# A six-layer cross network: the first layer's second half fed by a DMA transpose and multiplied in column tiles

## The chip, the cores and the metric

The kernel runs on one core of a Trainium2 chip. Five engines work side by side, each with its own queue: TensorE (PE in the profile, with PEld for its weight loads), VectorE (DVE), ScalarE (ACT), GpSimd (POOL) and SyncE (SP), which here only issues transfers. The metric is the time of one execution in microseconds of the device; the time before is a median of 130.95 us over 3 runs (130.82 to 131.1).

## The reference, cut to what matters

There are B = 4096 rows of D = 416 features (bf16), and L = 6 layers, each with a 416 x 416 matrix and a bias:

```
x = x0
for l in range(6):
    x = x0 * (x @ ws[l] + bs[l]) + x
return x
```

Each layer needs all of the layer before, so the layers come one after another, but the 4096 rows are independent of each other.

## The kernel before, in words

**Layout.** 416 features are 3 blocks of 128 and a remainder of 32. The kernel holds x transposed: in `XM`, the partitions are the features of one block and the free dimension is the 4096 rows. `XM[0]` is x0 and stays; `XM[1]` and `XM[2]` take turns. The remainder's 32 features of 4 groups of 512 rows are stacked on the 128 partitions of `XR`; `XRd` is a copy of it with the two halves of the partitions swapped, for products that would otherwise meet on the same rows of TensorE's array. The 4096 rows are two halves (`s` = 0 and 1), each of four groups (`g`) of 512 columns. The main weights are in `WM`, the remainder's rows of them in `WR` (four copies, one in each 32 partitions), and their 32 x 32 corners on a diagonal in `WD`.

**A product.** For layers 1 to 4, `mm_full` (L177) makes one 128 x 512 block of the result from three 128-feature blocks; it splits the 128 output features into four column tiles of 32 (`tile_position=(0, 32*q)`), so a group of four matmuls (L181) fills the array. `mm_row` (L185) adds the remainder's 32 input features with row tiles (L187), and `mm_rem` (L191) makes the remainder's 32 output features with column tiles (L193 for the diagonal corner, L198 for the main blocks). The first layer uses a `full` of its own (L211) that does the same as `mm_full` with single 128 x 128 matmuls (L214), and a `row` (L217, its matmul at L221) that reads `XRd` for the second block (m = 1).

**After a product.** `ew_main` (L162) adds the bias on ScalarE (L165) from PSUM to a scratch tile `t`, multiplies by x0 (L166) and adds x (L169) on VectorE. `ew_rem` (L171) does the same for the remainder (L173 to L175). PSUM is one pool of four buffers, each of two banks: a new product can start only when ScalarE has emptied one. The framework orders each engine's work mostly as the program text has it; `pin` and `keep_in_program_order` hold an operation at its place in the text.

**The first layer, `first_layer(s)` (L208), run for s = 0 and then s = 1.** First the products of groups 0 and 1 for the three feature blocks (`pa`), then their row products and the one that opens the next tile (eight matmuls, which need `XR` and, for m = 1, `XRd`), then groups 2 and 3 (`pb`) and the last four row products, then the remainder product `pr`. Between the two halves, `x0_rem(1, ...)` (L155) transposes the second half's remainder on TensorE (four matmuls against the identity, L157) into the free bank of `pr`, and VectorE copies it to `XR` and, swapped, to `XRd` (three copies, L160).

**How the inputs come.** SP's queue issues, in this order: the transposed loads of x0's first two groups (L76, a DMA transpose of 512 rows x 384 features each), the remainder's weights for layer 0 (L88), groups 2 and 3, group 0 of the second half, the second half's remainder `xrem` (L85, rows of 64 bytes), groups 1, 2 and 3 of the second half, and then the weights of the other layers (L72, L91) and x0 by rows (L125). ScalarE's queue issues layer 0's weights, the biases and the first half's remainder (`xrig`, L81). ScalarE copies `WR` twice (L110) and GpSimd once (L112); GpSimd fills `WD` (L131) and regroups `xrem` into `xrig` (L134), so that a transpose of 128 x 128 blocks brings the four groups where `XR` has them.

**Layers 1 to 4** run over six tiles (half, feature block) in pairs, with the remainder pair for both halves (`rem_pair`, L267) after the first pair. **The last layer** turns the product round: the 128 rows of a block are the stationary operand and the 416 features the moving one (`mm_q_full`, L325, its matmul at L327), so that the result comes out by rows; `mm_q_rem` (L330) adds the remainder (L333) and the bias (L336). Two blocks of 128 rows are opened ahead of the first bias product, then the rest follows in four rounds. ScalarE takes the result from PSUM (L354), VectorE multiplies by x0 (L355) and adds x (L344), and SP writes it out.

Of the kernel before, what the change touches and what calls it, by code (L numbers as in the profile page):

```python
# [11 lines left out]
BF16 = mybir.dt.bfloat16  # L12
# [4 lines left out]
def kernel(  # L17
# [65 lines left out]
    def load_xrem1():  # L83
        with nc.allow_non_contiguous_dma(reason="64B row segments"):
            nc.sync.dma_start(xrem[:], x0_v[:, 16:32, NK * P:D])  # L85
# [29 lines left out]
    load_x0t(1, 0)  # L115
    load_xrem1()
    for g in range(1, NG):
        load_x0t(1, g)
    load_wm(nc.sync, 1)
# [13 lines left out]
    fill_wd(0, 1)  # L133
    nc.gpsimd.tensor_copy(xrig[:, 1].rearrange("p i (g r) -> p i g r", g=NG), xrem[:].rearrange("p (g i) r -> p i g r", g=NG))  # L134
    fill_wd(1, L)
# [19 lines left out]
    def x0_rem(s, tpr):  # L155
        for i in range(4):
            nc.tensor.transpose(tpr[:, 128 * i:128 * i + 128], xrig[:, s, i, :], ident[:])  # L157
        for dst, src in ((slice(0, P), slice(0, P)), (slice(64, P), slice(0, 64)), (slice(0, 64), slice(64, P))):
            to = XR[0] if dst == src else XRd
            nc.vector.tensor_copy(to[dst, CW * s:CW * s + CW], tpr[src])  # L160
# [46 lines left out]

    def first_layer(s):  # L208
        cur, curR, nxt, nxtR = XM[0], XR[0], XM[1], XR[1]

        def full(pt, m, h, gl, after_row):  # L211
            c0 = col0(s, 2 * h + gl)
            for k in range(NK):
                nc.tensor.matmul(pt[:, gl, :], lhsT=WM[:, 0, k, 128 * m:128 * m + 128], rhs=cur[:, k, c0:c0 + CW],  # L214
                                 start=(k == 0 and not after_row), stop=(k == NK - 1 and after_row))
# [13 lines left out]
        if s == 0:  # L229
            for m in range(NK):  # L230
                full(pa[m], m, 0, 0, False)
            tp0 = psum.tile([P, CW], BF16, tag="ps", name="tpr")
            x0_rem(0, tp0[:])
            for m in range(NK):
                full(pa[m], m, 0, 1, False)
        else:
            for m in range(NK):
                for gl in range(2):
                    full(pa[m], m, 0, gl, False)
        pb = [ph(0)]  # L240
# [6 lines left out]
        for m in range(NK):  # L247
            if m:
                pb.append(ph(m))
            for gl in range(2):  # L250
                full(pb[m], m, 1, gl, m == 0)
        row(pb[1], 1, 1, False)
        row(pb[2], 2, 1, False)
        pr = psum.tile([P, 2, CW], FP32, tag="ps", name="pr")
        mm_rem(0, s, pr[:, 0, :], cur, curR)
        if s == 0:
            x0_rem(1, pr[:, 1, :].bitcast(BF16)[:, 0:CW])
        for m in range(NK):
            ew_main(0, s, m, 1, pb[m], cur, nxt, pin=(s == 0))
        ew_rem(0, s, pr[:, 0, :], curR, nxtR)  # L260

    bias_setup()
# [3 lines left out]

    def rem_pair(l, cur, curR, nxtR, feeds_last):  # L267
        pr2 = psum.tile([P, 2, CW], FP32, tag="ps", name="pr2")
        for s in range(NS):
            mm_rem(l, s, pr2[:, s, :], cur, curR)  # L270
        for s in range(NS):
            ew_rem(l, s, pr2[:, s, :], curR, nxtR)
            if feeds_last:
                nc.sync.dma_start_transpose(out=scrR[s][:], in_=nxtR[:, CW * s:CW * s + CW])
# [50 lines left out]
    def mm_q_full(q, g, py, closes):  # L325
        for k in range(NK):
            nc.tensor.matmul(py[:, 0:D], lhsT=cur[:, k, q_cols(q, g)], rhs=WM[:, l, k, :],  # L327
                             start=((not closes) and k == 0), stop=(closes and k == NK - 1))
# [34 lines left out]
    for q, at, done in rounds:  # L363
# [7 lines left out]
        for u in range(done):  # L371
            mm_q_full(q, u, bank[u], False)
# [40 lines left out]
```

## Time and profile before

| | |
|---|---|
| runs | 130.95 us median (130.82 to 131.1, 3 runs) |
| the profiled execution | 130.71 us, span 128.9 us, granted clock 0.998 |
| TensorE | 123.1 us busy (96% of the span), 1690 matmuls |
| VectorE | 107.1 us busy (83%) |
| ScalarE | 86.9 us busy (67%) |
| GpSimd | 5.9 us busy (5%) |
| transfers | 16.37 MB in 42102 packets, over 90% busy from about 3 to 38 us |

The span is the time from the first to the last instruction that the profiler saw; the execution's own time is 1.8 us longer. All times in the text are microseconds from the start of the span. The busy share of TensorE counts pipelined matmuls and is no measure of the array at its peak. The chain that ended last follows the execution back from its last instruction, at each step to what released it; it is the view to read for what a change is worth, since an engine's work beside the chain costs nothing.

### The profile page before, as it was taken

Reading aid. Unit: us, or ns where it says so; the run is one execution under the profiler, and the core shown is the slowest. Engines: PE = TensorE matmul, PEld = TensorE weight load, DVE = VectorE, ACT = ScalarE, POOL = GpSimd, SP = SyncE. Lnnn points to the kernel's source line nnn. Section 1 sums busy time; section 2 is a strip of 40 time slices with the busy share of each in tenths; the row PEclk is TensorE's granted clock in tenths of the full one; section 3 lists DMA queues with packets and bytes.
Section 4 is the critical chain, followed back from the end, with each engine's and each line's share of the span. In section 5 each row is a group of like instructions: output and inputs, shape, how many; then the busy total and the mean of one; then the engine's idle time right before and its main releaser. Section 6 shows DMA issues by size and latency. Waiting matters only on the chain.

```text
span 128.9 us, 3973 instructions
## 1 busy us (share of the span) xinstructions
PE 123.1 (96%) x1690; PEld 54.9 (43%) x1690; DVE 107.1 (83%) x197; ACT 86.9 (67%) x99; POOL 5.9 (5%) x18
## 2 busy tenths in 40 slices
PE   6999999999999999999999999999999999999960
PEld 2343443354444444444444444444444445445420
DVE  1032979999999898989898989898989899898991
ACT  0426783987848577848668848668847896569670
POOL 4022200600000000000000000000000000000000
PEclk9999999999999999999999999999999999999999
DMA  3999999999990000000000000000297999995754
GB/s 106 237 203 217 170 158 260 247 328 333 336 299 11 5 0 8 0 0 5 0 5 0 5 0 5 0 5 0 42 166 164 123 219 178 187 323 188 231 179 139
DMA packets 42102, 16.37 MB, mean 127 GB/s; under 512 B 30906, under 2 KB 42084, under 8 KB 42084
## 3 DMA queue, kind: packets, MB, share of 16 engines
q1 hardware_dynamic: 39416, 15.56, 54.6%
q10 hardware_dynamic: 2668, 0.56, 2.3%
q8 instruction: 13, 0.21, 0.7%
q14 instruction: 5, 0.04, 0.1%
HBM read 6.15 MB, written 3.41 MB: 74 GB/s over the span
## 4 chain that ended last, share of the span: by engine, by line
PE 80%; DMA 8%; DVE 5%; issue 2%; SPq 1%; ACT 1%; DVEq 0%
PE pt L181 49%; PE ph L214 9%; DMA XM<-in_x_dram 8%; PE py L327 8%; PE pt L187 5%; PE pr L198 5%; DVE t L355 3%; DVE o L344 2%; PE pr L193 2%; SPq L76 1%; PE py L333 1%; PE ph L221 1%; PE py L336 1%; ACT t L354 1%; PE pr L157 0%
## 5 line engine op out<-in xcount | busy, mean ns | idle before, releaser
L181 PE MATMUL pt<-XM,WM 128*32 128x512 bf16 x1152 | 65.2, 379 | 0.0
L165 ACT ACTIVATE t<-pt,bM 128x1024 bf16<-128x1024 f32 x48 | 49.6, 1115 | 18.3 <-PE pt L187 18.3
L166 DVE TENSOR_TENSOR t<-t,XM 128x1024 bf16<-128x1024 bf16 x60 | 41.4, 690 | 5.3 <-ACT t L165 5.3
L169 DVE TENSOR_TENSOR XM<-t,XM 128x1024 bf16<-128x1024 bf16 x60 | 41.8, 696 | 3.4
L181 PEld LDWEIGHTS <-WM 128*32 128x32 bf16 x1152 | 29.7, 97 | 33.8 <-issue 5.1
L354 ACT CAST t<-py 128x416 bf16<-128x416 f32 (+1 forms) x23 | 14.8, 642 | 4.8 <-PE py L327 2.1
L327 PE MATMUL py<-WM,XM 128*128 128x416 bf16 x96 | 17.7, 340 | 0.0
L214 PE MATMUL ph<-XM,WM 128*128 128x512 bf16 x72 | 16.5, 379 | 0.1
L165 ACT ACTIVATE t<-ph,bM 128x1024 bf16<-128x1024 f32 x12 | 12.5, 1114 | 4.4 <-PE ph L221 4.4
L327 PEld LDWEIGHTS <-XM 128*128 128x128 bf16 x96 | 9.0, 98 | 8.5 <-issue 1.4
L355 DVE TENSOR_TENSOR t<-t,X0rows 128x416 bf16<-128x416 bf16 (+1 forms) x23 | 10.4, 454 | 1.2 <-ACT t L354 1.2
L214 PEld LDWEIGHTS <-WM 128*128 128x128 bf16 x72 | 6.8, 98 | 8.6 <-issue 1.3
L344 DVE TENSOR_TENSOR o<-t,XLrows 128x416 bf16<-128x416 bf16 (+1 forms) x23 | 10.3, 451 | 0.0
L173 ACT ACTIVATE t<-pr,bR 128x512 bf16<-128x512 f32 x10 | 6.4, 684 | 2.7 <-PE pr L198 2.1
L198 PE MATMUL pr<-XM,WM 128*32 128x512 bf16 x120 | 8.2, 379 | 0.0
L187 PE MATMUL pt<-XR,WR 32*128 32x512 bf16 x96 | 7.3, 379 | 0.0
L141 PE MATMUL wps<-warm 128*128 128x512 bf16 (+1 forms) x11 | 4.4, 593 | 1.2 <-DVE warm L94 1.2
L175 DVE TENSOR_TENSOR XR<-t,XR 128x512 bf16<-128x512 bf16 x10 | 4.2, 423 | 0.7
L198 PEld LDWEIGHTS <-WM 128*32 128x32 bf16 x120 | 3.2, 97 | 3.1
L106 ACT ACT_TABLE_LOAD x1 | 1.3, 1283 | 4.3 <-DMA WM<-in_ws_dram 4.3
L174 DVE TENSOR_TENSOR t<-t,XR 128x512 bf16<-128x512 bf16 x10 | 4.2, 418 | 0.0
L152 DVE CAST bM<-pb 128x18 f32<-128x18 bf16 x1 | 0.2, 177 | 4.6 <-PE pb L151 4.6
(39 smaller groups left out, 33.6 us busy)
## 6 DMA issues: line engine op xcount, KB each, us to landing
X0rows<-in_x_dram SPq DMA_DIRECT2D x4, 832.0 KB, 11.6
out_dram<-o SPq DMA_DIRECT2D x9, 208.0 KB, 2.4
WM<-in_ws_dram SPq DMA_DIRECT2D x5, 312.0 KB
out_dram<-o SPq DMA_DIRECT2D x13, 104.0 KB, 1.7
WR<-in_ws_dram SPq DMA_DIRECT2D x4, 130.0 KB, 4.1
WM<-in_ws_dram ACTq DMA_DIRECT2D x1, 312.0 KB
XM<-in_x_dram SPq DMA_TRANSPOSE x8, 4.9
xrig<-in_x_dram ACTq DMA_DIRECT2D x4, 32.0 KB, 4.1
```

Of the source, the lines that this page charges most:

```text
L165: nc.scalar.activation(t[:], pt[:].rearrange("p a b -> p (a b)"), ACT.Identity, bias=bM[:, m, l:l + 1], scale=1.0)
L166: prod = nc.vector.tensor_tensor(out=t[:], in0=t[:], in1=XM[0][:, m, c0:c0 + 2 * CW], op=ALU.mult)
L169: nc.vector.tensor_tensor(out=nxt[:, m, c0:c0 + 2 * CW], in0=t[:], in1=cur[:, m, c0:c0 + 2 * CW], op=ALU.add)
L173: nc.scalar.activation(tr[:, 0:CW], pr, ACT.Identity, bias=bR[:, l:l + 1], scale=1.0)
L181: nc.tensor.matmul(pts[g // 2][32 * q:32 * q + 32, g % 2, :], lhsT=WM[:, l, k, 128 * m + 32 * q:128 * m + 32 * q + 32], rhs=cur[:, k, c0:c ...
L187: nc.tensor.matmul(pts[g // 2][:, g % 2, :], lhsT=WR[32 * g:32 * g + 32, l, 128 * m:128 * m + 128], rhs=curR[32 * g:32 * g + 32, CW * s:CW ...
L198: nc.tensor.matmul(pr[32 * g:32 * g + 32, :], lhsT=WM[:, l, k, NK * P:D], rhs=cur[:, k, c0:c0 + CW], start=False, stop=(k == NK - 1), tile ...
L214: nc.tensor.matmul(pt[:, gl, :], lhsT=WM[:, 0, k, 128 * m:128 * m + 128], rhs=cur[:, k, c0:c0 + CW], start=(k == 0 and not after_row), sto ...
L327: nc.tensor.matmul(py[:, 0:D], lhsT=cur[:, k, q_cols(q, g)], rhs=WM[:, l, k, :], start=((not closes) and k == 0), stop=(closes and k == NK ...
L344: tc.keep_in_program_order(nc.vector.tensor_tensor(out=o, in0=t, in1=xl, op=ALU.add))
L354: nc.scalar.copy(tv, src)
L355: tc.keep_in_program_order(nc.vector.tensor_tensor(out=tv, in0=tv, in1=X0rows[:, b, :], op=ALU.mult))
```

## The change

It touches only the first layer, the order of some transfers and the last layer's first products:

- `xrem` is issued on ScalarE's queue instead of SP's.
- The second half's remainder is transposed by a DMA from SBUF to SBUF, issued on SP after group 2 of the second half and ahead of group 3, straight into `XR[0]`; TensorE's four transposes and VectorE's copy to `XR` go. GpSimd's regrouping copy moves ahead of its fills of `WD`. The two copies into `XRd` stay on VectorE, pinned ahead of the product of the first half's third tile (`x0_rem1`).
- The second half's products (s = 1) use `mm_full`, that is, four column tiles for each single matmul.
- The two remainder products of the first layer are made together, by `rem_pair`, in the second half after the first tile of groups 2 and 3; `rem_pair` itself is the same and only stands earlier in the text.
- The elementwise work on the first half's groups 2 and 3 is emitted in the second half, after the first tile's products.
- In the last layer, the first two blocks of the first round are multiplied with the stationary 128 columns split into four column tiles of 32.

```diff
@@ -82,7 +82,7 @@
 
     def load_xrem1():
         with nc.allow_non_contiguous_dma(reason="64B row segments"):
-            nc.sync.dma_start(xrem[:], x0_v[:, 16:32, NK * P:D])
+            tc.keep_in_program_order(nc.scalar.dma_start(xrem[:], x0_v[:, 16:32, NK * P:D]))
 
     def load_wr0():
         nc.sync.dma_start(WR[0:R, 0, :], ws[0, NK * P:D, :])
@@ -112,10 +112,13 @@
             nc.gpsimd.tensor_copy(dst, src)
     for g in range(2, NG):
         load_x0t(0, g)
-    load_x0t(1, 0)
     load_xrem1()
-    for g in range(1, NG):
+    for g in range(NG - 1):
         load_x0t(1, g)
+    nc.gpsimd.tensor_copy(xrig[:, 1].rearrange("p i (g r) -> p i g r", g=NG), xrem[:].rearrange("p (g i) r -> p i g r", g=NG))
+    nc.sync.dma_start_transpose(out=XR[0][:, CW:2 * CW].rearrange("p (i c) -> p i c", i=4),
+                                in_=xrig[:, 1].rearrange("p i c -> p (i c)"))
+    load_x0t(1, NG - 1)
     load_wm(nc.sync, 1)
     for g in range(NG):
         load_wr(nc.sync, g, 1, L)
@@ -130,9 +133,8 @@
         for g in range(NG):
             nc.gpsimd.tensor_copy(WD[32 * g:32 * g + 32, l0:l1, g, :], WR[32 * g:32 * g + 32, l0:l1, NK * P:D])
 
-    fill_wd(0, 1)
-    nc.gpsimd.tensor_copy(xrig[:, 1].rearrange("p i (g r) -> p i g r", g=NG), xrem[:].rearrange("p (g i) r -> p i g r", g=NG))
-    fill_wd(1, L)
+    for l0, l1 in ((0, 1), (1, L)):
+        fill_wd(l0, l1)
 
     wps = psum.tile([P, CW], FP32, tag="ps", name="wps")
 
@@ -152,12 +154,18 @@
         nc.vector.tensor_copy(bM[:], pb[:, 0:NK, 0:L])
         nc.vector.tensor_copy(bR[:], pb[:, 3, 0:L])
 
-    def x0_rem(s, tpr):
+    HALVES = ((slice(64, P), slice(0, 64)), (slice(0, 64), slice(64, P)))
+
+    def x0_rem0(tpr):
         for i in range(4):
-            nc.tensor.transpose(tpr[:, 128 * i:128 * i + 128], xrig[:, s, i, :], ident[:])
-        for dst, src in ((slice(0, P), slice(0, P)), (slice(64, P), slice(0, 64)), (slice(0, 64), slice(64, P))):
-            to = XR[0] if dst == src else XRd
-            nc.vector.tensor_copy(to[dst, CW * s:CW * s + CW], tpr[src])
+            nc.tensor.transpose(tpr[:, 128 * i:128 * i + 128], xrig[:, 0, i, :], ident[:])
+        nc.vector.tensor_copy(XR[0][:, 0:CW], tpr)
+        for dst, src in HALVES:
+            nc.vector.tensor_copy(XRd[dst, 0:CW], tpr[src])
+
+    def x0_rem1():
+        for dst, src in HALVES:
+            tc.keep_in_program_order(nc.vector.tensor_copy(XRd[dst, CW:2 * CW], XR[0][src, CW:2 * CW]))
 
     def ew_main(l, s, m, h, pt, cur, nxt, pin=False):
         c0 = col0(s, 2 * h)
@@ -205,10 +213,22 @@
         nc.sync.dma_start_transpose(out=XLrows[:, 16 * s:16 * s + 16, 128 * k:128 * k + 128],
                                     in_=nxt[:, k, SW * s:SW * s + SW])
 
+    def rem_pair(l, cur, curR, nxtR, feeds_last):
+        pr2 = psum.tile([P, 2, CW], FP32, tag="ps", name="pr2")
+        for s in range(NS):
+            mm_rem(l, s, pr2[:, s, :], cur, curR)
+        for s in range(NS):
+            ew_rem(l, s, pr2[:, s, :], curR, nxtR)
+            if feeds_last:
+                nc.sync.dma_start_transpose(out=scrR[s][:], in_=nxtR[:, CW * s:CW * s + CW])
+
     def first_layer(s):
         cur, curR, nxt, nxtR = XM[0], XR[0], XM[1], XR[1]
 
         def full(pt, m, h, gl, after_row):
+            if s == 1:
+                mm_full(0, s, m, 2 * h + gl, {h: pt}, cur, not after_row, after_row)
+                return
             c0 = col0(s, 2 * h + gl)
             for k in range(NK):
                 nc.tensor.matmul(pt[:, gl, :], lhsT=WM[:, 0, k, 128 * m:128 * m + 128], rhs=cur[:, k, c0:c0 + CW],
@@ -230,13 +250,18 @@
             for m in range(NK):
                 full(pa[m], m, 0, 0, False)
             tp0 = psum.tile([P, CW], BF16, tag="ps", name="tpr")
-            x0_rem(0, tp0[:])
+            x0_rem0(tp0[:])
             for m in range(NK):
                 full(pa[m], m, 0, 1, False)
         else:
             for m in range(NK):
                 for gl in range(2):
                     full(pa[m], m, 0, gl, False)
+                if m == 0:
+                    for mm in range(NK):
+                        if mm == 2:
+                            x0_rem1()
+                        ew_main(0, 0, mm, 1, late[mm], cur, nxt, pin=True)
         pb = [ph(0)]
         row(pa[0], 0, 0, False)
         row(pb[0], 0, 1, True)
@@ -249,29 +274,21 @@
                 pb.append(ph(m))
             for gl in range(2):
                 full(pb[m], m, 1, gl, m == 0)
+            if s == 1 and m == 0:
+                rem_pair(0, cur, curR, nxtR, False)
         row(pb[1], 1, 1, False)
         row(pb[2], 2, 1, False)
-        pr = psum.tile([P, 2, CW], FP32, tag="ps", name="pr")
-        mm_rem(0, s, pr[:, 0, :], cur, curR)
         if s == 0:
-            x0_rem(1, pr[:, 1, :].bitcast(BF16)[:, 0:CW])
+            late.extend(pb)
+            return
         for m in range(NK):
-            ew_main(0, s, m, 1, pb[m], cur, nxt, pin=(s == 0))
-        ew_rem(0, s, pr[:, 0, :], curR, nxtR)
-
+            ew_main(0, s, m, 1, pb[m], cur, nxt)
+
+    late = []
     bias_setup()
     pe_filler(1, CW)
     for s in range(NS):
         first_layer(s)
-
-    def rem_pair(l, cur, curR, nxtR, feeds_last):
-        pr2 = psum.tile([P, 2, CW], FP32, tag="ps", name="pr2")
-        for s in range(NS):
-            mm_rem(l, s, pr2[:, s, :], cur, curR)
-        for s in range(NS):
-            ew_rem(l, s, pr2[:, s, :], curR, nxtR)
-            if feeds_last:
-                nc.sync.dma_start_transpose(out=scrR[s][:], in_=nxtR[:, CW * s:CW * s + CW])
 
     def xl_rem(s):
         tc.keep_in_program_order(
@@ -322,8 +339,14 @@
         c = col0(s, g) + 128 * i
         return slice(c, c + 128)
 
-    def mm_q_full(q, g, py, closes):
+    def mm_q_full(q, g, py, closes, split=False):
         for k in range(NK):
+            if split:
+                c0 = q_cols(q, g).start
+                for r in range(4):
+                    nc.tensor.matmul(py[32 * r:32 * r + 32, 0:D], lhsT=cur[:, k, c0 + 32 * r:c0 + 32 * r + 32], rhs=WM[:, l, k, :],
+                                     start=((not closes) and k == 0), stop=(closes and k == NK - 1), tile_position=(0, 32 * r))
+                continue
             nc.tensor.matmul(py[:, 0:D], lhsT=cur[:, k, q_cols(q, g)], rhs=WM[:, l, k, :],
                              start=((not closes) and k == 0), stop=(closes and k == NK - 1))
 
@@ -369,7 +392,7 @@
             ew(q + u // 4, u % 4, n, tiles[tl][:, a:a + n, 0:D], nc.scalar if q + 2 == NQ and u == 7 else nc.sync)
 
         for u in range(done):
-            mm_q_full(q, u, bank[u], False)
+            mm_q_full(q, u, bank[u], False, split=(q == 0))
         mm_q_rem(q, bank[0:4], done)
         close(0, done)
         mm_q_rem(q + 1, bank[4:8], 0)
```

## The prediction

> **What bounds the kernel now.** I read the busy times first (TensorE 96% of the span, VectorE 83%), then the chain that ended last, because a share over the whole span does not say which stage could be shorter. In the chain, the stretch that the change touches is this (start, duration, engine and line, count):
>
> ```profile
> 12.14 3.40 PE ph L214 x15
> 15.54 0.33 PE ph L221 x4
> 15.87 0.33 PE pr L193 x4
> 16.20 0.65 PE pr L198 x12
> 16.85 0.33 PE pr L157 x4
> 17.18 3.88 PE ph L214 x18
> 21.06 0.54 PE ph L221 x8
> 21.61 3.99 PE ph L214 x18
> 25.60 0.33 PE ph L221 x4
> 25.92 0.33 PE pr L193 x4
> 26.25 0.65 PE pr L198 x12
> 26.90 2.59 PE pt L181 x48
> 29.49 0.54 PE pt L187 x8
> 30.03 2.71 PE pt L181 x48
> 32.74 0.21 PE pr L193 x4
> ```
>
> Each piece begins where the one before ends, so from 12.14 us on TensorE waits for nothing, and what is taken from its stream is taken from the end. Three prices stand here. A full 128x512 product takes 3.88/18 = 0.216 us, and four column tiles of 32 take 2.59/12 = 0.216 too: column tiling costs no pace. A change of tile shape costs 0.11: the first L181 piece follows column tiles (2.59), the second follows row tiles (2.71); L193 takes 0.33 after row tiles and 0.21 after column tiles. The four transposes of L157 take 0.22 and one such switch.
>
> The other end, from the same chain:
>
> ```profile
> 101.14 2.70 PE pt L181 x48
> 103.85 1.16 PE py L327 x6
> 105.01 0.29 PE py L333 x4
> ...
> 105.83 4.33 PE py L327 x24
> ...
> 115.81 0.86 ACT t L354
> ```
>
> TensorE leads up to 115.8, and then ScalarE and VectorE run the last two rounds behind each other. VectorE still idled 0.43 us at 116.69, waiting for ScalarE, which had waited 0.67 for a bias product (L336). So the tail starts when TensorE lets it, and up to about 0.43 us of an earlier TensorE passes through; beyond that VectorE's own queue is next.
>
> What feeds the stretch is SP's queue:
>
> ```profile
> 10.83 0.58 SPq L85 DMA_DIRECT2D xrem<-in_x_dram  x1
> 11.45 6.47 SPq L76 DMA_TRANSPOSE XM<-in_x_dram  x3
> 17.97 1.35 SPq L72 DMA_DIRECT2D WM<-in_ws_dram  x1
> ```
>
> The transposed loads of the second half (call them B0 to B3) are issued at 9.04, 11.45, 14.18 and 15.90. The trace's landing records put them at 13.95, 17.13, 19.93 and 21.27, and xrem at 15.14. TensorE needs B1 0.65 after the second half begins (17.83) and B3 0.65 into its second part (22.26): neither is late now, by 0.7 and 1.0 us.
>
> **The change on TensorE.** Before, 15.87 to 29.49 is 13.62 us. After, the order is: 18 groups of column tiles behind row products, 3.88 + 0.11 = 3.99; eight row products, 0.54; six groups, 1.29 + 0.11 = 1.40; both halves' remainder products, 1.73 (layer 1 does the same pair from 32.74 to 34.47); 12 groups, 2.59; four row products, 0.33; layer 1's first 48, now behind row tiles, 2.70. Sum 13.28. **Gain 0.34**: four transposes (0.22) and one switch (0.11). In the last layer the first six products, as column tiles, follow column tiles: 6 x 0.176 (4.22/24) = 1.05 instead of 1.16, **gain 0.11**. The doubt is the pace of four loads and four products in 0.176 us, since column tiles are shown only at 0.216. But the bias products L336 do eight instructions in 0.18. At 0.216 the six would take 1.30, a loss of 0.14; I take 0.11, by the nearer row. Together 0.45.
>
> **What was cover and is gone.** The removed 1.31 us (remainder product, transposes) stood ahead of the second half, which now starts at 15.87 instead of 17.18. So B1 is needed at 16.52, the transposed remainder XR at 19.86, its swapped copy XRd at about 20.3, and B3 at 15.87+3.99+0.54+0.11+0.65 = 21.16. Call the end of the eight row products E: planned 20.40; with the 0.11 of the last layer, the time is unchanged at E = 20.85.
>
> *B1.* xrem leaves SP, so B1 is issued at 10.83, 0.62 earlier; its issue took 2.68 where its neighbours took 1.75 and 1.68, and its packets flowed only after those of xrem. If only 0.62 is saved it lands at 16.5; if the long issue goes too, at 15.6. Both meet 16.52: cost 0. If nothing is saved, 17.13 costs 0.6. A rule of the Trainium skill speaks against a larger gain: in DMA: Bandwidth & Descriptors, section Issuing engines are not separate DMA queues, all queues share the same engines, and a second issuer saves only issue time. By it B1 lands at 16.55 and the sum is 0.03 less; the 2.68 of the row would say more, and no trace here shows xrem on the other queue.
>
> *xrem on ScalarE.* ScalarE's two copies of WR end at 9.92 and its next work starts at 11.09; the issue (0.58 on SP) fits in that idle 1.17. Landing: 4.1 (xrig, ScalarE's queue) to 4.3 (xrem) gives 14.1 to 14.3; the longest landing among these loads, 6.4, gives 16.4. GpSimd's copy is 0.79 plus about 0.1: done at 15.0 to 17.3. I take 15.1. The WD fill behind it on GpSimd (0.99) is first needed by the remainder pair at 21.8, so over 4 us cover it.
>
> *The transposed remainder.* It stands on SP behind B2, whose issue ends at 14.3 to 15.2. Price: the same shape, scrR, took 1.22 to issue and 2.5 to land; a whole load took 4.9. From 15.1 it lands between 17.6 and 20.0; from 17.3, at 22.2 at worst. I take 18.5: the load ahead may still be moving. XRd needs two copies (0.86) and a handover, so E = XR + 1.2, and 18.5 is early by 0.7. VectorE stands before those copies, and the pinned product of the third tile waits behind them; it reaches them at about 19.2 (16.6, plus two tiles at 1.33), so it waits for nothing, and layer 1 needs that tile at 26.5. VectorE is also relieved of one 0.42 copy.
>
> *B3, and what SP holds behind the wait.* B3 is issued at 15.1 + 1.2 = 16.3 instead of 15.90. With 4.9 (the median) it lands at 21.2, with 4.3 at 20.6, with its own 5.4 at 21.7: against 21.16 that costs 0, 0 and 0.5. I take 21.2: cost 0.04. Layer 1's weights and WR follow some 0.4 us later; WM landed at 22.36 and is needed at 26.5, WR at about 25 and GpSimd's fill at 25.9 are needed at 29 and 32. Scratch buffers: the pair's needs a first-part buffer that ScalarE empties by 21.4, at 21.8; if it is late, TensorE waits that long.
>
> **Sum.** 0.34 + 0.11 - 0.04, rounded to 0.40. The profiled execution took 130.71 us (span 128.9), 0.24 below the median 130.95. The span would be 128.5 and the median 130.55.
>
> **Rivals.** (1) *The remainder comes late.* Between xrem and the row products now stand a landing, GpSimd's copy, an SP wait, a transfer and two VectorE copies in series. It decides once XR lands after 19.65 (E = 20.85). With xrem at 15.1 as now, the copy done at 16.05 and a landing of 4.9, XR comes at 21.0, E = 22.2, and the kernel is 1.35 slower (132.3); with half that, 131.6. For it: the transfer engines are over 90% busy here, and instruction loading makes a hole. One packet of queue q8 (16 KB) falls between 17.5 and 18.5, and the rate drops from 297 GB/s (17.5 to 18.0) to 128, 77, 24 and 115 in the half microseconds from 18.0 to 20.0; B2 landed at 19.93 for it. About 190 TensorE instructions had then run; column tiles run eight per 0.216 us, so that point comes at about 17.2. XR in that hole lands at about 19.3, E = 20.5: 0.1 lost. The Trainium skill, in Runtime: NRT & Kernel Launch, section Instruction fetch mechanics, has refills of 256 instructions by a queue of the engine's own, mostly hidden; the 16 KB agree, and for the transposes beside it the hidden part does not. Against the rival: from 15.1, even 4.4 is in time. Chance 0.27 for over 0.2% slower.
> (2) *B1, XR or B3 costs 0.2 to 0.7* and eats the gain: B3 with its present 5.4 and a start 0.15 later gives E = 21.1, 131.2; with 5.2, E = 20.74 and 130.84. I give the cases within 0.2% 0.19.
> (3) *It does not do what it says*: B3 is put ahead of the remainder on SP, or xrem ahead on ScalarE. B3 first puts the remainder at 16.5 to 17, landing at 19.5 to 21.5, like rival 1: its 0.04 is in those 0.27.
> (4) *The last layer's tiles run at 0.216*: the sum falls to 0.15, 130.8. 0.05, inside the 0.19.
>
> **Chances.** A measurement of this kernel tells about 0.2% (0.26 us) from no change. Forecast, a gain over 0.26: 0.54, 130.3 to 130.69; within 0.26: 0.19; slower: 0.27, up to 132.3. The range 130.3 to 131.6 leaves out the worst half of rival 1 (0.12) and a little below, where no row shows a further gain.
>
> **What the profile would show.** No L157 at 16.85; column tiles of the second half beginning at about 15.9; layer 1's first L181 at about 26.5; L327 x24 and then L333 at about 0.4 earlier, and VectorE's idle at 116.7 nearly gone. Wrong if TensorE has a hole before the row products (XR, XRd) or 0.65 into the second part (B3), or if the tail begins earlier but ends the same.

## The result and the profile after

The changed kernel takes 131.54 us (median, 130.97 to 131.94); the kernel before takes 131.0 on the same chip (130.51 to 131.45). The ratio is 1.0038, with a 95% interval of 1.0022 to 1.0054. By the bound of the prediction (0.2%) that is slower, by about 0.50 us; the forecast was 0.40 faster. The profiled execution took 131.72 us (span 129.9), 0.18 above its median, where that of before lay 0.24 below its own: 0.42 of the 1.0 us between the two spans is the choice of executions.

The chain that ended last, in the changed kernel (start, duration, engine and line, count; SPq is SP's queue):

```profile
11.48 2.73 SPq L76
...
14.26 1.49 SPq L76
...
15.86 4.96 DMA XR<-xrig
...
20.86 0.71 PE ph L241 x8
21.57 1.56 PE ph L189 x24
...
27.78 2.70 PE pt L189 x48
30.48 0.54 PE pt L195 x8
```

Before, the chain was TensorE's alone from 12.14 on. Now it goes through SP's queue and a transfer up to 20.86: the eight row products (L241) wait for the transposed remainder XR. XR's input was ready at 15.04, when GpSimd's copy ended, but SP was still issuing the load ahead of it until 15.75; from its issue at 15.86 the transfer then took 4.96. Layer 1's row products begin at 30.48 instead of 29.49.

TensorE's timeline of the same stretch (idle time ahead of a piece, and its releaser, in brackets):

```profile
15.83 0.83 PE L189 MATMUL ph<-XM,WM 128*32 128x512 bf16 x12
17.14 3.42 PE L189 MATMUL ph<-XM,WM 128*32 128x512 bf16 x60 [0.47 <-DMA XM<-in_x_dram]
20.86 0.61 PE L241 MATMUL ph<-XR,WR 32*128 32x512 bf16 x6 [0.30 <-DMA XR<-xrig]
...
21.50 1.63 PE L189 MATMUL ph<-XM,WM 128*32 128x512 bf16 x24
```

Three waits stand here. The first three groups of tiles take 0.65, so the fourth should start at 16.48; it starts at 17.14: **B1, 0.66**. The fifteen groups then take 3.36 (so in the run e5 below, where nothing interrupts them), and the row products are due at 20.50; they start at 20.86: **XR, 0.36**, and they take 0.64 instead of 0.54, which is **XRd, 0.10**. Of the last piece the fourth group starts, by the trace's single records, at 22.30 instead of 22.16: **B3, 0.14**. Together 1.26. A wait costs more than its idle time in brackets: 0.47 of idle became 0.66 of delay. A product's record lasts 0.379, while in a running stream the next product starts 0.216 after it, so an idle time that is counted from the end of the last record leaves out about 0.16 of the delay.

The start of the second half lies 0.03 later than before (15.83 for 15.80). So 0.03 + 1.26 - 0.34 = 0.95, against 30.48 - 29.49 = 0.99 seen. At the other end, with the last layer's tiles (chain of the changed kernel):

```profile
104.84 1.05 PE py L347 x24
...
116.69 0.86 ACT t L377
```

The six products take 1.05 instead of 1.16, and ScalarE's piece starts at 116.69, not 115.81: 0.88 later, which is 0.99 less that 0.11.

### The profile page after: what moved, and what is told of

Its sections match the earlier page's. It is cut to its first block, busy times and chain, and to the rows that moved or that the text cites. A ratio compares the mean times of both kernels' runs of the same rounds, so it can differ in the third digit from the quotient of the medians.

```text
span 129.9 us, 4219 instructions
## 1 busy us (share of the span) xinstructions
PE 123.0 (95%) x1812; PEld 56.0 (43%) x1812; DVE 107.0 (82%) x196; ACT 86.7 (67%) x99; POOL 6.3 (5%) x18
## 3 DMA queue, kind: packets, MB, share of 16 engines
q1 hardware_dynamic: 37896, 15.56, 54.2%
## 4 chain that ended last, share of the span: by engine, by line
PE 74%; DMA 8%; SPq 7%; DVE 5%; issue 2%; ACT 1%; DVEq 0%
PE pt L189 49%; SPq L76 7%; PE py L350 7%; PE pt L195 5%; PE pr L206 5%; DMA XM<-in_x_dram 4%; DMA XR<-xrig 4%; DVE t L378 3%; PE ph L189 3%; DVE o L367 2%; PE pr L201 2%; PE py L356 1%; PE py L347 1%; PE ph L241 1%; PE py L359 1%
## 5 line engine op out<-in xcount | busy, mean ns | idle before, releaser
L189 PEld LDWEIGHTS <-WM 128*32 128x32 bf16 x1296 | 33.7, 97 | 38.1 <-issue 6.8
L350 PE MATMUL py<-WM,XM 128*128 128x416 bf16 x90 | 16.5, 339 | 0.0
L350 PEld LDWEIGHTS <-XM 128*128 128x128 bf16 x90 | 8.5, 98 | 7.8 <-issue 1.4
L189 PE MATMUL ph<-XM,WM 128*32 128x512 bf16 x144 | 8.7, 380 | 0.5 <-DMA XM<-in_x_dram 0.5
L234 PE MATMUL ph<-XM,WM 128*128 128x512 bf16 x36 | 8.3, 379 | 0.1
L234 PEld LDWEIGHTS <-WM 128*128 128x128 bf16 x36 | 3.4, 97 | 4.2 <-issue 0.4
L206 PEld LDWEIGHTS <-WM 128*32 128x32 bf16 x120 | 3.3, 97 | 3.2
```

The lines of the kernel that those rows point to most:

```text
L189: nc.tensor.matmul(pts[g // 2][32 * q:32 * q + 32, g % 2, :], lhsT=WM[:, l, k, 128 * m + 32 * q:128 * m + 32 * q + 32], rhs=cur[:, k, c0:c ...
L206: nc.tensor.matmul(pr[32 * g:32 * g + 32, :], lhsT=WM[:, l, k, NK * P:D], rhs=cur[:, k, c0:c0 + CW], start=False, stop=(k == NK - 1), tile ...
```

## The experiments

Fourteen kernels, each timed in five rounds against the kernel before on the same chip. The landing of a transfer is read from the trace's landing records. The trace of each kernel in the table holds one packet of 16 KB on queue q8 (its kind is "instruction") among the loads of the first 20 us; it is called the refill here.

| kernel | ratio to before, 95% | refill at | what landed late, and TensorE's idle time for it |
|---|---|---|---|
| before | 1 | 17.84 | B2 (19.93): none, it is needed last of its half |
| after | 1.0038 [1.0022, 1.0054] | 18.97 | XR (20.82): 0.30; B1 (17.09): 0.47 |
| e1_no_rem_load | 1.0014 [0.9993, 1.0035] | 19.00 | B3 (21.41): below 0.2 |
| e2_rem_on_sp | 1.0086 [1.0054, 1.0117] | 19.29 | B3 (22.81): 0.27; B1 (17.81): 0.66 |
| e3_rem_on_te | 1.0031 [1.0010, 1.0053] | 19.60 | B3 (21.99): 0.44 |
| e4_by_group | 1.0012 [0.9992, 1.0032] | 18.05 | XR (20.44): 0.52 |
| e5_fill_after | 1.0063 [1.0035, 1.0091] | 15.56 | B1 (17.59): 1.25 |
| e6_fill_te | 1.0037 [1.0016, 1.0059] | 15.78 | B1 (17.81): 0.23 |
| e7_fill_before | 1.0060 [1.0038, 1.0082] | 16.34 | B1 (19.09): 0.90 |
| e8_split_before | 1.0004 [0.9984, 1.0025] | 18.76 | B2 (20.81): none |
| e9_no_tiles | 1.0059 [1.0040, 1.0077] | 19.44 | B3 (22.47): 0.71 |
| e10_no_tiles_by_group | 1.0064 [1.0040, 1.0087] | 18.91 | B3 (22.11): 0.77 |
| e11_no_tiles_refill_back | 1.0038 [1.0019, 1.0057] | 17.72 | XR (20.47): 0.73 |
| e12_te_refill_mid | 0.9996 [0.9979, 1.0013] | 17.73 | B2 (19.80): none |

The profiles also differ from each other by chance: the first half's own fourth group of rows is late by 0 to 0.78 us, in kernels of either kind. So single profiles tell which transfer is late; how much a kernel loses is read from the ratios, and kernels that were timed on different chips are compared by their ratios too.

### Where the arrivals cost

**e1_no_rem_load.** The changed kernel without the second half's remainder load, its regrouping and its transposition; VectorE copies the first half's remainder in its place, so that the second half's remainder is left out of the result.

```diff
-    load_xrem1()
...
-    nc.gpsimd.tensor_copy(xrig[:, 1]..., xrem[:]...)
-    nc.sync.dma_start_transpose(out=XR[0][:, CW:2 * CW]..., in_=xrig[:, 1]...)
...
+        for r in (XR[0], XRd):
+            nc.vector.tensor_copy(r[:, CW:2 * CW], r[:, 0:CW])
```

> The changed kernel without the load, regrouping and transpose of the second half's remainder: VectorE fills that half of XR and XRd from the first half's (this part of the result is left out). Theory A (the change frees 0.45 us of TensorE, and the second half's inputs come too late for it: the load B1, the remainder and B3 hold TensorE for about 0.5, 0.5 and 0.15): with 128 KB less to move and no transpose on SP, B1 lands at about 15.8 and B3 at about 20, TensorE has no hole after 12.1, layer 1 begins at about 26.5, and the kernel is 0.35 to 0.5 faster than before. Theory B (the column tiles, the common remainder pair and the delayed elementwise work cost something themselves): layer 1 begins at 27 or later without any wait for a transfer, and the kernel is no faster than before.

Measured: 1.0014 [0.9993, 1.0035]. SP's issue of B1 in its chain:

```profile
11.05 1.98 SPq L76
```

It took 1.98 where it takes 2.73 with xrem beside it, and B1 landed at 16.26 instead of 17.09. The row products then begin at 19.94 and the next tiles at 20.48, as the prediction had planned for 19.86 and 20.40. In the other kernels of the table, which all have xrem, the issue of B1 takes 2.5 to 3.0, so the longer issue is the remainder load's doing. B1's landing is less clear: with the same transfers ahead of it and no refill near, it is 16.44 to 17.09 in the changed kernel, e3, e4 and e9 to e12. What still was late is B3: its packets had all been moved at 19.27, but the refill stood at 19.00, and the landing came at 21.41. That delays TensorE by 0.32 (the fourth group of the next tiles starts at 21.45 instead of 21.13), and the gain of 0.35 to 0.5 that was expected is not seen.

**e2_rem_on_sp.** xrem back on SP, behind B0; all else as changed.

```diff
-            tc.keep_in_program_order(nc.scalar.dma_start(xrem[:], ...))
+            nc.sync.dma_start(xrem[:], ...)
...
+    load_x0t(1, 0)
     load_xrem1()
-    for g in range(NG - 1):
+    for g in range(1, NG - 1):
```

> The changed kernel with xrem back on SP's queue behind B0, all else as changed. Theory A: the same bytes go through the same engines, so B1 lands at about 17.1 as in both kernels, the remainder's transpose is issued at about 16.0 and lands at about 20.9: as slow as the changed kernel, within 0.2. Theory C (the move to ScalarE's queue is what costs, since its 64-byte packets run beside B0): B1 and the remainder come earlier, and the kernel is at least 0.3 faster than the changed one.

Measured: 1.0086 [1.0054, 1.0117]. Both expectations were missed: it is 0.6 us slower than the changed kernel by the ratios, whose intervals touch. The waits are for B1 (0.66) and B3 (0.27), not for XR, which lands at 19.79. The first half's fourth group was late by 0.56 in this profile, so the landings compare poorly with those of the changed kernel; the ratio speaks for ScalarE's queue as the better of the two places.

**e3_rem_on_te.** TensorE transposes the second half's remainder, at the start of the second half; the DMA transposition goes, and the rest of the change stays.

```diff
-    nc.sync.dma_start_transpose(out=XR[0][:, CW:2 * CW]..., in_=xrig[:, 1]...)
...
+        if s == 1:
+            x0_rem(1, tp1[:])    # four transposes, three copies on VectorE
```

> The changed kernel with the second half's remainder transposed on TensorE again, at the start of the second half, and three copies on VectorE; no DMA transpose of it; xrem stays on ScalarE's queue. Theory A: TensorE pays 0.33 more, which lies beside the wait for B1, the wait for the remainder is gone and B3 comes about 1 us earlier: E, the end of the eight row products, at about 20.9, and the time is that of before, within 0.2, so 0.3 to 0.6 faster than the changed kernel. Theory B: still 0.3 or more slower than before.

Measured: 1.0031 [1.0010, 1.0053]; the time of before, which theory A expected, was missed. Neither B1 (landed 16.82) nor the remainder holds TensorE by more than 0.1. TensorE's timeline has one wait left:

```profile
22.03 0.83 PE L187 MATMUL ph<-XM,WM 128*32 128x512 bf16 x12 [0.44 <-DMA XM<-in_x_dram]
```

This is B3. It was issued at 15.68, its last packet was moved at 19.86, and it landed at 21.99; the refill stood at 19.60. Here no DMA transposition is ahead of B3, so SP's order is not the cause.

**e4_by_group.** The changed kernel, with the second half's first part by groups: group 0 for the three blocks, then group 1, so that B1 is needed 1.3 us later.

```diff
-            for m in range(NK):
-                for gl in range(2):
-                    full(pa[m], m, 0, gl, False)
-                if m == 0:
+            for gl, m in ((gl, m) for gl in range(2) for m in range(NK)):
+                full(pa[m], m, 0, gl, False)
+                if (gl, m) == (0, 0):
```

> The changed kernel with the first part of the second half taken by groups (all three feature blocks of group 0, then all of group 1), so that B1 is needed 1.3 us later. Theory A: the wait for B1 (0.47) is gone, but the remainder still lands at about 20.8 and TensorE waits for it the longer: E and the time as in the changed kernel, within 0.15. Theory D (the waits add up): 0.47 faster than the changed kernel, so equal to before.

Measured: 1.0012 [0.9992, 1.0032], about 0.34 us faster than the changed kernel by the ratios, with intervals that overlap; theory A had expected no change beyond 0.15. The wait for B1 is gone, and the waiting moved to XR (0.52). XR came at 20.44 and not at 20.82, with a refill at 18.05. So a gain, if it is one, may be the order or where the refill fell; this run alone doesn't divide them. It does show that B1's wait is not what sets the end of the row products: without it TensorE waits for XR.

### Moving the refill

After e1, e3 and e4 a second theory stood beside the plain sum of arrivals: a refill of TensorE's instructions delays the transposed load that is under way when it comes, and the change moved it from a load with time to spare (B2) onto one without (XR). The way to test it is to move the refill alone. The fillers at the start of the kernel (matmuls on a constant, whose results nothing reads) were cut into more and smaller ones with the same number of columns in all: 36 of 128 columns are 52 more TensorE instructions, products and weight loads, than 2 of 256 and 8 of 512.

**e5_fill_after, e6_fill_te, e7_fill_before.** The changed kernel, e3 and the kernel before, with one edit:

```diff
-    pe_filler(2, 2 * P)
-    pe_filler(8, CW)
+    pe_filler(36, P)
```

> The changed kernel with the ten warm-up products ahead of the input (2 of 256 and 8 of 512 columns) cut into 36 of 128: the same columns, 52 more TensorE instructions ahead of everything. Theory H (the transposed transfers in flight when TensorE's instruction refill, the 16 KB packet of q8, comes land 1 to 2 us late): the refill comes at 17.0 to 17.7 instead of 18.97, falls on B2 instead of the remainder, and XR lands at 19.5 to 20.5 instead of 20.8: 0.3 to 0.6 faster than the changed kernel. Theory Q (the queue of transfers is simply too long, wherever the refill falls): XR at 20.8, the same time as the changed kernel within 0.15.

> The kernel of e3 (remainder transposed on TensorE) with the same 36 fillers. In e3 the refill came at 19.60 and B3, whose packets had moved by 19.9, landed at 21.99 and cost TensorE about 0.6. Theory H: the refill comes at about 18.2, B3 lands at 20.8 to 21.3 where it is needed at 21.4, and the kernel is 0.4 to 0.6 faster than e3: 0.1 to 0.2 faster than before. Theory Q: B3 at about 22, the time of e3 within 0.15.

> The kernel before with the same 36 fillers, to see what the fillers do by themselves. The refill comes 52 instructions earlier, at about 15.8 instead of 17.84 (TensorE runs fewer instructions in a microsecond here), and falls on B1, which may land at 17.5 to 18 where it is needed at 17.83. Theories H and Q: the same time as before within 0.2; a gain over 0.2 would mean that the fillers help by something else than the refill, and e5 and e6 would prove nothing.

Measured: 1.0063 [1.0035, 1.0091], 1.0037 [1.0016, 1.0059] and 1.0060 [1.0038, 1.0082]. The refills came earlier than expected, at 15.56, 15.78 and 16.34, so they met B1 in all three, and the numbers expected were missed. e7 is the cleanest run of the study: it is the kernel before, with no transfer and no product but the fillers changed, and it is 0.6% slower. Its refill comes 1.5 us earlier than that of before, so the packet does go with TensorE's instructions. TensorE's timeline in e7 (of an execution 0.52 above its median), and below it the half microseconds of the same stretch (after the length come the busy times of TensorE, its weight loads, VectorE, ScalarE and GpSimd; the last three columns are the granted clock, the DMA share and GB/s):

```profile
17.42 0.81 PE L213 MATMUL ph<-XM,WM 128*128 128x512 bf16 x3
19.13 3.40 PE L213 MATMUL ph<-XM,WM 128*128 128x512 bf16 x15 [0.90 <-DMA XM<-in_x_dram]
```

```profile
16.00:16.50 0.50, 0.50 (x12) 0.19 (x12) 0.46 (x1) 0.19 (x1) 0.11 (x1) 1.00 1.22 266
16.50:17.00 0.50, 0.50 (x16) 0.15 (x8) 0.00 (x0) 0.50 (x1) 0.50 (x1) 1.00 4.11 27
17.00:17.50 0.50, 0.50 (x13) 0.32 (x6) 0.00 (x0) 0.50 (x2) 0.00 (x1) 1.00 0.04 4
...
18.00:18.50 0.50, 0.23 (x2) 0.00 (x0) 0.46 (x2) 0.43 (x1) 0.00 (x0) 1.00 1.11 245
```

The rate falls from 266 GB/s to 27, 4 and (in the half microsecond left out) 10, right behind the refill at 16.34, and returns to 245 at 18.0. B1, which lands 5.67 after its issue in before, takes 7.23 here (issued at 11.86, landed at 19.09). The changed kernel has such a hole about 2 us later (the two half microseconds left out have 111 and 121 GB/s):

```profile
18.00:18.50 0.50, 0.50 (x16) 0.31 (x12) 0.50 (x2) 0.06 (x1) 0.00 (x0) 1.00 1.40 272
18.50:19.00 0.50, 0.50 (x16) 0.29 (x12) 0.47 (x2) 0.00 (x0) 0.00 (x0) 1.00 0.51 90
...
20.00:20.50 0.50, 0.50 (x12) 0.07 (x5) 0.00 (x0) 0.00 (x0) 0.00 (x0) 1.00 0.08 9
```

XR is in it: by the trace's packets its data had been moved by 18.71, but its landing records run from 19.10 to 20.82.

The landing records show the refill better than the rate does. Each of these transfers has sixteen, and the last one releases the engine that waits. Of XR's, eleven come by 19.23 and five from 20.78 on, a gap of 1.55. In nine of the fourteen profiles of the table the load that is under way at the refill has such a gap, of 1.08 to 1.64 us (before's B2, e1's and e3's B3 and e5's B1 among them), and no other of B0 to B3 and XR has one over 0.87. In the other five all sixteen records come together; there e7's B1 and e11's B2 take the longest of their kind from issue to landing (7.23 and 6.16), while the B3 of e2, e9 and e10 takes no longer than elsewhere. The rate alone is no sign: in e1 and e3, where loads of weights follow, it stays at 235 GB/s or more in the microsecond behind the refill, and in the changed kernel it is down to 58 from 16.0 to 16.5, where no refill is.

**e9_no_tiles, e10_no_tiles_by_group, e11_no_tiles_refill_back.** The other way to move the refill: single 128 x 128 products in the second half instead of column tiles, a quarter of the instructions. e10 adds the order of e4, e11 adds 24 fillers of 192 columns (28 more instructions) to e10.

```diff
         def full(pt, m, h, gl, after_row):
-            if s == 1:
-                mm_full(0, s, m, 2 * h + gl, {h: pt}, cur, not after_row, after_row)
-                return
```

> The changed kernel with the second half's products as single 128x128 matmuls again (two TensorE instructions where the column tiles issue eight); everything else as changed. Theory H: the 193rd TensorE instruction is reached only at about 21, so the refill comes after the loads; XR lands at about 19.2 and B3 at about 21, and only the wait for B1 (0.66) is left. TensorE's own work is 0.12 + 0.11 less than before, so the kernel is 0.4 slower than before at most and 0.1 to 0.4 faster than the changed one. Theory Q: XR still at 20.8, no faster than the changed kernel.

> e9 with the first part of the second half taken by groups as in e4, so that B1 is needed 1.3 us later. Theory H: no wait for B1, XR or B3 above 0.2 in all; 0.1 to 0.25 faster than before and 0.6 faster than the changed kernel. Theory Q: XR at 20.4 to 20.8 and the time of e4.

> e10 with the ten warm-up products cut into 24 of 192 columns: 28 TensorE instructions more, which bring the refill back to about 18. Theory H: it falls on B2 and the remainder, XR lands at 20 to 20.5, and the kernel is 0.4 to 0.7 slower than e10, with the same work after the warm-up. Theory Q: the time of e10 within 0.15.

Measured: 1.0059 [1.0040, 1.0077], 1.0064 [1.0040, 1.0087] and 1.0038 [1.0019, 1.0057]; all three numbers were missed. The refill of e9 came at 19.44, not about 21, and of e10 at 18.91, so it met B3 in both (idle 0.71 and 0.77), while XR landed in time, at 18.50. B3 was also issued late there, at 17.30 (15.90 in before), and these runs don't divide the two causes. In e11 it came at 17.72 and the hole passed to XR (20.47, idle 0.73); B3, at 21.72, was in time. e11 was expected slower than e10 and is 0.47 us faster by the medians, with intervals that overlap. What answers to the refill is the landing of XR: from its issue it takes 2.42 to 2.44 in e9 and e10, where the refill comes after its landing, and in e14, where it comes before its issue (16.65), and 4.59 to 5.04 in the changed kernel, e4 and e11, where one falls on it or on B2 just ahead. e2 is an exception: its refill came 0.37 ahead of XR's first record, and XR took only 2.86. The time at which the refill comes was guessed badly.

**e12_te_refill_mid.** e3 with the 24 fillers of 192 columns, meant to put the refill on B2, the load with time to spare.

```diff
-    pe_filler(2, 2 * P)
-    pe_filler(8, CW)
+    pe_filler(24, 192)
```

> e3 (remainder transposed on TensorE, so that its 0.33 us lie in the wait for B1) with 24 fillers of 192 columns: between e3, where the refill came at 19.60 on B3, and e6, where it came at 15.78 on B1. Theory H: the refill comes at 17 to 18.5 and falls on B2, which has slack; B3 lands at 20.8 to 21.3 where it is needed at 21.4; 0.3 to 0.6 faster than e3 and within 0.2 of before, or 0.1 faster. Theory Q: the time of e3 (131.3).

Measured: 0.9996 [0.9979, 1.0013], 0.46 us faster than e3 by the ratios, whose intervals barely overlap, with 28 instructions more. The refill stood at 17.73 and B2 landed at 19.80, needed later. The chain of e12 is TensorE's alone again:

```profile
15.95 0.33 PE tpr L158 x4
16.27 4.08 PE ph L186 x72
20.36 0.54 PE ph L238 x8
20.90 1.41 PE ph L186 x24
```

No piece is longer than its products. This is the best version with the changed order of products that the runs found, and it equals the kernel before, which fits its sum: from 15.95 to layer 1's row products at 29.66 are 13.71, 0.09 more than the 13.62 of before, and the last layer gives 0.11 back.

### TensorE's own part

**e8_split_before.** The kernel before with only the last layer's column tiles (the last hunk of the change).

> The kernel before with only the last layer's part of the change (the first two blocks' products as four column tiles). Theory A: the six products take 1.05 instead of 1.16 and the tail begins 0.11 earlier: 0.1 faster than before, too little to be told from no change by its time, but to be read in the chain. Rival: four column tiles of 416 columns take 0.216, and it is 0.14 slower.

Measured: 1.0004 [0.9984, 1.0025]. A gain of 0.11 us is 0.08%, below what can be seen here; the piece itself is 1.05 instead of 1.16 in the profile.

**e13_no_loads_before, e14_no_loads_after.** Both kernels without the loads B0 to B3: the second half's x0 is a constant, set by GpSimd and VectorE, so the second half's results are left out. Then no such load can be late.

```diff
     def load_x0t(s, g):
         c0 = col0(s, g)
+        if s == 1:
+            for k in range(NK):
+                (nc.vector if k == 2 else nc.gpsimd).memset(XM[0][:, k, c0:c0 + CW], 0.05)
+            return
```

> The kernel before without the four loads of the second half (its columns of x0 are filled with a constant on GpSimd and VectorE, so its results are left out). All theories: TensorE has no hole after the first half's loads as before, so the same time as before within 0.3; it is the partner of e14.

> The changed kernel without the same four loads (its results for the second half are left out); the remainder's load, regrouping and DMA transpose stay. Theory A: with nothing ahead of it on SP the remainder lands before 19.2, TensorE has no hole in the second half, layer 1 begins 0.45 earlier than in e13 and the tail 0.45 earlier: e14 is 0.35 to 0.5 faster than e13. Theory B (the column tiles, the pair or the delayed elementwise work cost something of their own): no faster than e13.

Measured: 131.22 us, 1.0033 [1.0021, 1.0044], and 130.64 us, 0.9981 [0.9966, 0.9995], on one chip. Both were expected to have no wait, and e13 the time of before within 0.3; it is 0.43 slower, and each pays one wait of its own for the remainder. In e13 GpSimd regroups xrem late, at 16.09, behind its fills, and the step from the remainder product to the second half's first product takes 1.57 instead of 1.21 (0.36). In e14 xrem itself lands at 16.59, with loads of weights beside it, XR is issued at 17.43, the row products start 0.23 late, at 19.89 for 15.66 + 4.00, and XRd costs 0.11. TensorE's timeline of e13, and below it that of e14:

```profile
15.87 0.60 PE L197 MATMUL pr<-XR,WD 128*32 128x512 bf16 x4
...
17.44 4.05 PE L218 MATMUL ph<-XM,WM 128*128 128x512 bf16 x18
...
29.85 0.61 PE L191 MATMUL pt<-XR,WR 32*128 32x512 bf16 x8
```

```profile
15.66 4.07 PE L193 MATMUL ph<-XM,WM 128*32 128x512 bf16 x72
19.89 0.61 PE L245 MATMUL ph<-XR,WR 32*128 32x512 bf16 x6 [0.17 <-DMA XR<-xrig]
...
29.29 0.61 PE L199 MATMUL pt<-XR,WR 32*128 32x512 bf16 x8
```

From 15.66 to 29.29 are 13.63, less 0.34 for the waits 13.29; e13 has 13.98 (15.87 to 29.85), less 0.36, 13.62. The prediction had 13.28 and 13.62. The medians differ by 0.58, where 0.45 was the sum; the waits nearly cancel. So TensorE's gain is real, and what the changed kernel loses, it loses to arrivals.

## Why the prediction was wrong, step by step

**TensorE's sum (0.34 + 0.11): right.** e13 and e14 give 0.33 in the first layer, and the last layer's piece went from 1.16 to 1.05. The rival that those tiles run at 0.216 (1.30) falls.

**B1 (cost 0): failed, 0.66 in the profiled execution.** It rested on B1 being issued earlier once xrem left SP's queue. It was issued at 11.48, as late as before (11.45): the issue of B0 began 0.40 later (9.44 for 9.04) and took 2.00 instead of 1.74. B1's own issue took 2.73 (2.68 before). xrem's packets, now on ScalarE's queue, ran beside B0 from 10.98 to 13.70, and B0 landed at 14.99 instead of 13.95. The rule of the Trainium skill that it cited (DMA: Bandwidth & Descriptors, section Issuing engines are not separate DMA queues) leaves a second issuer the saving of issue time; here the 0.62 that xrem's issue had taken on SP was used up by the later and longer issue of B0. In e1, without xrem, B1 lands at 16.26, between the two bounds that the prediction gave (15.6 and 16.5). With xrem, fifteen of B1's sixteen landing records are there by 16.23 as well, and the last comes at 17.09. What held that one back no run shows. The removed cover of 1.31 was then missing, and B1 cost 0.66. The prediction had this case as its bound ("if nothing is saved, 17.13 costs 0.6") and did not choose it.

**xrem on ScalarE: right, and not what decides.** It was issued at 9.15 between ScalarE's copies, and GpSimd's copy was done at 15.04, where 15.1 was taken. (GpSimd ran the first of its fills of `WD` ahead of that copy after all, at 9.84; this cost nothing.) But SP was not free to issue the transposition: B2's issue ended at 15.75.

```profile
15.86 1.35 SPq L119 DMA_TRANSPOSE XR<-xrig  x1
17.26 1.51 SPq L76 DMA_TRANSPOSE XM<-in_x_dram  x1
```

**XR (taken 18.5): this is the step that decides the time, and rival 1 had its mechanism.** SP's timeline has the issue at 15.86, not 15.1, and the landing came 4.96 later, at 20.82. The time in flight is the larger part of the error. In the chain of e14, whose refill comes before XR's issue, the same transfer takes 2.42:

```profile
17.43 2.42 DMA XR<-xrig
```

In e9 it is issued later than in the changed kernel, at 16.06, and lands at 18.50, the very value taken. In the changed kernel the refill came at 18.97, just ahead of XR's first landing record, and held five of the sixteen back to 20.78 and later. The prediction had seen such a hole on B2 and placed the next one at 17.2, by a count of about 190 TensorE instructions, with XR at 19.3 in it; in the changed kernel 240 had run by the refill. XR alone sets the end of the row products: with B1 in time they could not have started before 20.82 either (in e4, without B1's wait, they start at 20.48, right behind XR at 20.44). So E is 21.50 instead of the planned 20.40, 1.10 later, of which the waits for B1, XR and XRd are the parts. Rival 1's price of 1.35 counted E as XR + 1.2; it is XR + 0.68 here, because the two copies into XRd take 0.61 instead of 0.86 and run beside the row products that need XR alone. A late B1 with XR in time would have cost 0.66 by itself, which is also more than the gain of 0.45.

**B3 (cost 0.04).** It was issued at 17.26 instead of 16.3 and landed at 22.26; since TensorE was late as well, it cost 0.14.

**What else was claimed.** VectorE did wait, 1.27 at 20.84, for XR, which the prediction excluded for a landing at 18.5; GpSimd's fills, layer 1's weights and the PSUM buffers hold nothing. VectorE's idle ahead of the tail, expected to vanish, is 0.42 at 117.58 (0.43 before): TensorE was later and not earlier.

**The sum.** Gains of 0.45 and waits of 1.26 give 0.81 slower in the profiled execution; the medians say 0.50 (0.29 to 0.71 by the interval). The measured 131.54 lies in the stated range, 0.06 below its upper end; the range reached so far because of rival 1 and not because of the sum, so its holding is no credit to the forecast of a gain. The chance of 0.27 for slower was too small: it rested on a refill at 17.2, and in the fourteen profiles of the table the refill lies between 15.56 and 19.60. The 1.31 us taken from TensorE's path had covered such delays: B1 landed no later than before (17.09 for 17.13), and was late only because it was needed earlier.

**What stays open.** That a refill delays a transposed load under way is shown most clearly by e7 against before, in the landing and in the time. In e12 against e3 and in e11 against e10 the landings move with the refill, but the intervals of the times overlap; e2's XR was not delayed. By what mechanism a landing is held, and why B1's last record was late in the changed kernel, no run shows. No run has the changed kernel with the refill out of the way: e4 moves it onto B2, and XR behind it still comes at 20.44; e5 moves it onto B1. When the refill comes was predicted only roughly: in the traces 169 to 280 TensorE instructions, products and weight loads, had been executed by then. No version was found that beats the kernel before by more than its interval, apart from e14, which leaves loads out.

## What to carry to other kernels

Work that is taken from the path of the bounding engine may have been the cover of a transfer: put the landings beside the new times of need, and take "the landing stays where it is" as the forecast unless a row shows the transfer's packets, and not only its issue, moving earlier. Look for instruction packets in a stretch that is full of transfers, and see which load they fall on; adding some tens of instructions to an engine far ahead moved it by 1 to 4 us here. On a load with time to spare, as B2 in the kernel before and in e12, the refill cost nothing.

## What the runs showed of the hardware

- A refill of 16 KB during transposed loads held part of the landing of the one under way for 1.08 to 1.64 us in nine of fourteen profiles; the rate fell with it where other transposed loads followed (from 266 GB/s to 27 and 4 in e7) and stayed at 235 or more where loads of weights followed (e1, e3). The Trainium skill (Runtime: NRT & Kernel Launch, section Instruction fetch mechanics) calls the cost of a refill mostly hidden; it is so for TensorE, which didn't stop for it, and not for the loads that TensorE waits for: e7 has 52 tiny instructions more than before and is 0.6% slower.
- A transposed load can have moved all its packets and still land 2.1 us later (e1's B3: 19.27 and 21.41; e3's: 19.86 and 21.99). In both, fifteen of the sixteen landing records were there by 19.77 and 20.34; one was late, and TensorE waits for the last. Moved bytes are not a landing.
- SP's issue of the transposed loads B0 to B3 took 1.49 to 2.73 us in the changed kernel. B1's took 1.98 without xrem's packets beside the load ahead (e1) and 2.5 to 3.0 with them: time in the issuing queue depends on what is being moved.
- An idle gap of TensorE inside a stream of products costs about 0.16 to 0.19 more than the profile's idle time (0.47 became 0.66, e7's 0.90 became 1.06), because that is counted from the end of a record of 0.379 whose successor would have started after 0.216.
